# A fused transformer block on one core: the q projection of two row chunks as one Strassen pair, and a layer norm moved to ScalarE

## The chip, the cores and the metric

The kernel runs on one core of a Trainium2 chip. The metric is the device time of one execution in microseconds. Before the change it is 770.38 us, the median of 3 runs (770.19 to 770.63).

## The reference

2048 rows of 1024 numbers in bf16 go through a pre-norm block. Attention is local: each position looks at 8 positions, 2 apart, at and before itself, with 32 heads of 32. The feed-forward part is bilinear: gate times up, with no activation function between.

```python
x = A_x
h = x + _A_ref(_layernorm(x), A_wqkv, A_wo)    # x @ wqkv (1024 x 3072), attention, @ wo (1024 x 1024)
h2 = h + _B_ref(_layernorm(h), B_w_gate, B_w_up, B_w_down)   # (x @ wg) * (x @ wu), then @ wd; F = 3584
```

## The kernel before, in words

**Chunks and groups.** The rows are cut into 4 chunks of 512. `lnTs[c]` is the normalized chunk, transposed: 8 blocks (KO) of 128 channels by 512 rows. The weight wqkv comes in 6 blocks of 512 columns: blocks 0 and 1 are q, 2 and 3 k, 4 and 5 v. A *group* is `mm_group` (L429 to L432): 8 matmuls of 128x128 by 128x512 into one of the 8 PSUM banks. `qkv(c, blocks)` (L434) runs 4 groups for each block; `evac_qkv` (L342) then lets ScalarE copy the bank into a row buffer (pool `t1k`, 30 of them) and, for k and v, add the last 16 columns of the chunk before (`halo`), and SP stores it to DRAM. For q, `m` counts the 8 groups of 128 columns, and m below 8 means q.

**Attention** (`attention`, L468) is VectorE's work but for one exponential. It reads q and k back from DRAM in another order (`load_qk`, L448, issued on POOL's queue: qD, kD), later v (vD), and writes its output oD to DRAM, from where four DMAs on POOL's queue bring it back transposed as oT (L536 to L539). The chunks' attentions follow one another. `wo` of a chunk (8 groups that read oT) adds the residual row tiles `hss[c]`, and the second norm follows.

**The order of the work.** Everything is queued in the order of the program text; each engine works off its own queue in that order. TensorE's groups are written out by hand at the end of this section's listing. All else is a list of Python generators in `Background` (L37). Each `bg.step(us)`, one after each group with GROUP_US = 1.73, adds credit, up to 4; while the credit is positive, the first ready generator of the list is advanced. What it yields is charged in microseconds of VectorE's time; a pair `("later", us)` costs nothing, but puts it off. `bg.spend` charges work that is queued directly, and `bg.finish` runs a generator out. `pump`, `retire` and `state["live"]` load weight blocks in the order of `stream` into 7 buffers of pool `w`.

**The lines concerned.** Chunk 0's first block of q is done ahead of all. Then come `qkv(0, range(1, 4))`; the read of chunk 0's q and k; `qkv(1, range(4))`; v of chunk 0 and of chunk 1; `qkv(2, range(6))`; q and k of chunk 3; `wo_ln2(0)`, the output projection of chunk 0 with its second norm; v of chunk 3; and `ffn1_first`, gate and up of chunk 0, in which after 18 of 28 pairs of groups wo of chunk 1 is inserted (`wo_1`, `wo_norm`). Chunk 1's and chunk 2's first norms are `rows_gen` (statistics on VectorE, their Ln and Exp on ScalarE at L187 and L188), of which chunk 1's last two transposes are issued on ScalarE's own queue (L231). Chunk 3's first norm and chunk 1's second are `NormOnScalar` (L259): sums, squares and rows all on ScalarE. `wo_ln2` (L589) has its statistics (L183) and its normalization (L192) on VectorE.

**Strassen in the kernel.** Later stages already multiply 2x2 blocks with 7 products in place of 8 (`pair_block`, L829; the down projection from L1044 on), with f16 operands. `Scale` (L628) sums absolute weights on ScalarE and, with one matmul against ones (`total`, L642), gives each partition a power of two that keeps the f16 values in range.

Of the kernel before, what the change touches and what calls it, by code (L numbers as in the profile page):

```python
# [78 lines left out]
def kernel(  # L79
# [45 lines left out]
    bg = Background()  # L125

# [132 lines left out]
    class NormOnScalar(Norm1):  # L259
# [16 lines left out]
        def devs(self):  # L276
            nc.scalar.activation(self.nm, self.s, ACTF.Copy, scale=-1.0 / D)
            for t in range(4):
                nc.scalar.activation(self.junk[:], self.xs[t][:], ACTF.Square, bias=self.nm[:, t:t + 1],
                                     accum_out=self.ss[:, t:t + 1])  # L280
                yield "later", self.pace
            nc.scalar.activation(self.rs4[:], self.ss, ACTF.Ln, bias=eps[:], scale=1.0 / D)
# [17 lines left out]
        def rows(self):  # L300
            for t in range(4):
                self.row(t)
                self.transpose(t)
                yield "later", self.pace

# [33 lines left out]

    qkv_in = {}  # L340

    def evac_qkv(c, m, ps):  # L342
        sg = t1k.tile([128, HB + TC], BF, tag="t1k", name=f"sg{c}_{m}")
        nc.scalar.copy(sg[:, HB:HB + TC], ps[:])  # L344
# [5 lines left out]
        if m < 8:  # L350
            nc.sync.dma_start(qd[c][:, 4 * hg:4 * hg + 4, :, :].rearrange("c g d s -> (g d) c s"),
                              sg[:, HB:HB + TC].rearrange("p (c s) -> p c s", c=4))
            return
# [80 lines left out]
    def qkv(c, blocks, last=False):  # L434
        for b in blocks:
            for j in range(4):
                ps = psum.tile([128, TC], F32, tag="mm", name=f"ps{c}_{b}_{j}")
                mm_group(ps, wts["qkv", b], j, lnTs[c])
# [111 lines left out]
    class Norm2(NormOnScalar):  # L550
# [11 lines left out]
        def finish(self):  # L562
            yield from self.devs()
# [5 lines left out]
    def wo_norm(c):  # L569
# [4 lines left out]
        for t in range(4):  # L574
            for hf in range(2):
# [6 lines left out]
                if hf == 0 and t > 0:  # L582
                    n.sum(t - 1)
                bg.step(GROUP_US)
        n.sum(3)
        retire(2)
        return n

    def wo_ln2(c, at={}):  # L589
        lnT = lnTp.tile([128, KO, TC], BF, tag="lnT", name=f"lnT2_{c}")  # L590
        hs = hss[c]
        mv4, rs4 = ln_tiles(f"2_{c}")

        def norm(t):
            ln = normalize(hs[t], mv4, rs4, t)
            nc.sync.dma_start_transpose(lnT[:, :, bass.ts(t, 128)], ln[:])

        for t in range(4):
            for hf in range(2):
                ps = psum.tile([128, 512], F32, tag="mm", name=f"wo{c}_{hf}_{t}")  # L600
                for kk in range(KO):
                    nc.tensor.matmul(ps[:], lhsT=oTs[c][:, kk, t, :], rhs=wts["wo", c, hf][:, kk, :],
                                     start=(kk == 0), stop=(kk == KO - 1))
# [314 lines left out]
    def f16(ap):  # L918
        return ap.bitcast(F16)
# [434 lines left out]
```

## Time and profile before

| what | us |
| --- | --- |
| median of 3 runs | 770.38 |
| the profiled execution | 770.53 |
| its span, from the first to the last instruction | 768.7 |
| TensorE busy (3663 matmuls) | 762.8 |
| VectorE busy | 606.0 |
| ScalarE busy | 513.1 |
| GpSimd busy | 142.5 |
| matmul groups of q, k and v from 27.20 us on, without a gap | 136.41 |
| wo of chunk 0 starts | 163.61 |
| ffn1 of chunk 0 starts | 191.24 |
| wo of chunk 1 starts | 253.40 |

The span differs from the execution's time by what lies around the first and the last instruction, 1.8 us. "Idle before" and the name in brackets in a timeline say how long an engine stood still and what ended that. PE is TensorE, DVE VectorE, ACT ScalarE, POOL GpSimd, SP the engine that issues most DMAs; PEld is the load of the stationary operand, which lies beside the matmuls. A line such as L431 is the line of the kernel before.

### The profile page before, as it was taken

The numbers are of one execution on the slowest core, as the hardware profiler recorded it, in microseconds if no ns is written. First come the engines' busy times: TensorE is split into PE (matmuls) and PEld (weight loads), VectorE is DVE, ScalarE is ACT, GpSimd is POOL, SyncE is SP. The second block draws the span as 40 slices with busy tenths as digits, with TensorE's granted clock in tenths as the row PEclk, the third lists the DMA queues.
The fourth block names the chain that finished last, engine by engine and source line by source line (L and its number), as shares of the span: only waits on it lengthen the run. The fifth ranks groups of instructions, "written<-read, shape, count | busy, mean of one in ns | idle before, by whom it ended". The sixth has DMA issues, their size and how long they took to land.

```text
span 768.7 us, 10302 instructions
## 1 busy us (share of the span) xinstructions
PE 762.8 (99%) x3663; PEld 350.7 (46%) x3663; DVE 606.0 (79%) x718; ACT 513.1 (67%) x979; POOL 142.5 (19%) x152
## 2 busy tenths in 40 slices
PE   8999999999999999999999999999999999999998
PEld 5444444444444444444444444444444444444444
DVE  5639999999999999999998997975454444568863
ACT  4648966423687398778899986736777677788240
POOL 0000000200002000020000001018778677600000
PEclk9999999999999999999999999999999999999999
DMA  8999796999966699579559448674342423730001
GB/s 268 272 257 260 207 269 153 279 305 283 301 219 216 210 299 294 172 246 326 194 186 300 139 155 279 126 198 107 80 110 55 110 74 91 257 126 29 0 29 55
DMA packets 190915, 144.85 MB, mean 188 GB/s; under 512 B 81808, under 2 KB 181136, under 8 KB 188688
## 3 DMA queue, kind: packets, MB, share of 16 engines
q1 hardware_dynamic: 180416, 116.94, 54.2%
q0 software_dynamic: 3584, 22.02, 8.4%
q10 hardware_dynamic: 6864, 5.24, 2.5%
q8 instruction: 28, 0.46, 0.2%
q14 instruction: 23, 0.19, 0.1%
HBM read 110.10 MB, written 27.26 MB: 179 GB/s over the span
## 4 chain that ended last, share of the span: by engine, by line
PE 97%; DVE 2%; DMA 1%; issue 0%; ACTq 0%; DVEq 0%
PE ps L431 21%; PE dx L944 6%; PE pz L826 6%; PE pwu L431 6%; PE pu L431 6%; PE py L826 6%; PE pwg L431 6%; PE pg L431 6%; PE px L826 6%; PE wo L998 4%; PE pv L826 3%; PE ez L944 3%; PE ey L944 3%; PE ex L944 3%; PE dy L944 3%; PE wo L578 2%
## 5 line engine op out<-in xcount | busy, mean ns | idle before, releaser
L431 PE MATMUL ps<-lnT,w_qkv 128*128 128x512 bf16 x736 | 159.5, 379 | 0.0
L431 PEld LDWEIGHTS <-w_qkv 128*128 128x128 bf16 x736 | 71.9, 98 | 86.1 <-issue 0.2
L344 ACT CAST sg<-ps 128x512 bf16<-128x512 f32 x96 | 55.2, 586 | 46.9 <-PE ps L431 41.6
L477 DVE TENSOR_TENSOR prod<-qD,kD 128x4096 bf16<-128x4096 bf16 x32 | 72.2, 2284 | 12.8 <-DMA kD<-kd 12.8
L523 DVE TENSOR_TENSOR pv<-vD,at 128x4096 bf16<-128x4096 bf16 x32 | 72.4, 2285 | 0.2
L826 PEld LDWEIGHTS <-sw 128*128 128x128 f16 x448 | 43.8, 98 | 52.9 <-issue 0.2
L431 PEld LDWEIGHTS <-w_wu 128*128 128x128 bf16 x448 | 43.8, 98 | 52.9
L431 PEld LDWEIGHTS <-w_wg 128*128 128x128 bf16 x448 | 43.8, 98 | 52.9
L826 PE MATMUL px<-lnT,ws 128*128 128x512 bf16 x224 | 55.2, 379 | 0.0
L536 POOL DMA_DIRECT2D od<-oD x4 | 2.2, 544 | 275.6 <-DVE oD L534 275.6
L431 PE MATMUL pg<-lnT,w_wg 128*128 128x512 bf16 x224 | 52.9, 379 | 0.0
L431 PE MATMUL pu<-lnT,w_wu 128*128 128x512 bf16 x224 | 52.9, 379 | 0.0
L431 PE MATMUL pwu<-lnT,w_wu 128*128 128x512 bf16 x224 | 52.9, 379 | 0.0
L431 PE MATMUL pwg<-lnT,w_wg 128*128 128x512 bf16 x224 | 52.9, 379 | 0.0
L826 PEld LDWEIGHTS <-ws 128*128 128x128 f16 x336 | 32.9, 98 | 39.6
L807 POOL TENSOR_TENSOR sw<-ws 128x512 f16<-128x512 f16 x26 | 30.0, 1155 | 82.4 <-PE pv L826 49.1
L944 PEld LDWEIGHTS <-gs 128*128 128x128 f16 (+1 forms) x280 | 27.4, 98 | 33.0
L479 DVE TENSOR_TENSOR prod<-prod 128x4096 bf16<-128x4096 bf16 x16 | 36.6, 2288 | 0.4
L843 ACT COPY py<-px 128x512 f32<-128x512 f32 x28 | 16.0, 570 | 27.7 <-PE px L826 27.7
L808 POOL TENSOR_TENSOR sw<-sw,ws 128x512 f16<-128x512 f16 x26 | 30.0, 1154 | 2.0
L810 POOL TENSOR_TENSOR sw<-ws,sw 128x512 f16<-128x512 f16 x26 | 30.3, 1167 | 0.0
L809 POOL TENSOR_TENSOR sw<-ws 128x512 f16<-128x512 f16 x26 | 30.1, 1156 | 0.0
(334 smaller groups left out, 1472.9 us busy)
## 6 DMA issues: line engine op xcount, KB each, us to landing
w_wg<-in_B_w_gate_dram SPq DMA_DIRECT2D x14, 1024.0 KB, 6.9
w_wu<-in_B_w_up_dram SPq DMA_DIRECT2D x14, 1024.0 KB, 6.3
w_pair<-in_B_w_gate_dram SPq DMA_DIRECT2D x14, 512.0 KB, 4.0
w_pair<-in_B_w_up_dram SPq DMA_DIRECT2D x14, 512.0 KB, 5.3
w_wo<-in_A_wo_dram SPq DMA_DIRECT2D x6, 1024.0 KB, 7.6
w_qkv<-in_A_wqkv_dram SPq DMA_DIRECT2D x5, 1024.0 KB, 11.5
kd<-sg SPq DMA_DIRECT2D x32, 144.0 KB, 4.4
kD<-kd POOLq DMA_DIRECT2D x4, 1152.0 KB, 8.6
```

The source lines that it names most:

```text
L344: nc.scalar.copy(sg[:, HB:HB + TC], ps[:])
L431: nc.tensor.matmul(ps[:], lhsT=wt[:, ko, bass.ts(j, 128)], rhs=rhs[:, ko, :], start=(ko == 0), stop=(ko == KO - 1))
L477: nc.vector.tensor_tensor(prod[:, j], qD[:], kD[:, :, o:o + SUB], ALU.mult)
L479: nc.vector.tensor_tensor(prod[:, :, 0:16], prod[:, :, 0:16], prod[:, :, 16:32], ALU.add)
L523: nc.vector.tensor_tensor(pv[:, j], vD[:, :, o:o + SUB], at[:, w, None, :].to_broadcast((128, DH, SUB)), ALU.mult)
L807: eng.tensor_tensor(sw[:, i, 0], a21, a22, ALU.add)
L808: eng.tensor_tensor(sw[:, i, 1], sw[:, i, 0], a11, ALU.subtract)
L809: eng.tensor_tensor(sw[:, i, 2], a11, a21, ALU.subtract)
L810: eng.tensor_tensor(sw[:, i, 3], a12, sw[:, i, 1], ALU.subtract)
L826: nc.tensor.matmul(ps[:], lhsT=lhs[:, ko, :], rhs=rhs[:, ko, :], start=(fresh and ko == 0), stop=(ko == 3), skip_group_check=not fresh)
L944: nc.tensor.matmul(ps[:, bass.ds(lo, n)], lhsT=lhs[k][:, bass.ts(q, 128)], rhs=rhs[k][:, bass.ds(lo, n)], start=(fresh and k == 0), stop=( ...
L998: nc.tensor.matmul(ps[:], lhsT=oTs[c][:, kk, t, :], rhs=wts["wo", 2, hf][:, kk, :], start=(kk == 0), stop=(kk == KO - 1))
```

## The change

1. q of chunks 2 and 3 is taken out of `qkv` and computed together after wo of chunk 0 (`q_pair`, twice). The 2x2 blocks are: on the weights' side, block 0 or 1 of wqkv by the lower or upper half of the channels; on the rows' side, the half of the channels by chunk 2 or 3. For each m from 0 to 3 there are 7 products of 4 matmuls.
2. For that the q weights are converted in place to f16 with a scale (`q_abs` on ScalarE, 4 passes among the groups of chunk 0's k; `scale_q.rows`, `scale_q.total`, `q_convert`), right behind chunk 2's first norm. Their 16 block sums (`q_weight_sums`) go for m = 0 and 1 into 4 tiles of the row tiles' pool `hp`, for m = 2 and 3 into 8 row buffers of `t1k`. Chunk 1's q uses the converted weights and is scaled back in its eviction.
3. The rows' sums (`q_row_sums`) are made by VectorE during wo of chunk 0; one is written over a part of `lnTs[3]`.
4. `wo_ln2` is gone; chunk 0 uses `wo_norm(0, devs=False)`, with each row tile's sum, mean and squares on ScalarE as soon as that tile is added, and the rest in `finish(devs=False)` while the pair runs.
5. The order: chunk 1's k comes before its q; `start_attention(0)` stands ahead of the end of chunk 2's norm; loads of x of chunk 3, of weight blocks 4 and 5, and chunk 2's transposes stand behind the first block of chunk 1; chunk 3's norm is one generator (`both`). Attentions 2 and 3 are entered after the pair.

The core of the diff (`Scale` only moves up; `f16` too):

```diff
     def evac_qkv(c, m, ps):
-        nc.scalar.copy(sg[:, HB:HB + TC], ps[:])
+        if c == 1 and m < 8:
+            nc.scalar.activation(sg[:, HB:HB + TC], ps[:], ACTF.Copy, scale=scale_q.inv)
+        else:
+            nc.scalar.copy(sg[:, HB:HB + TC], ps[:])
...
+        def sum_dev(self, t):
+            col = slice(t, t + 1)
+            self.sum(t)
+            nc.scalar.activation(self.nm[:, col], self.s[:, col], ACTF.Copy, scale=-1.0 / D)
+            nc.scalar.activation(self.junk[:], self.xs[t][:], ACTF.Square, bias=self.nm[:, col],
+                                 accum_out=self.ss[:, col])
-        def finish(self):
-            yield from self.devs()
+        def finish(self, devs=True):
+            if devs:
+                yield from self.devs()
+            else:
+                yield "later", 2.0
+                self.sum_dev(3)
+                yield "later", self.pace
+                self.rstds()
+                yield "later", self.pace
             yield from self.rows()
...
-                if hf == 0 and t > 0:
+                if hf == 0 and t > 0 and devs:
                     n.sum(t - 1)
+                if hf == 1 and t > 0 and not devs:
+                    n.sum_dev(t - 1)
                 bg.step(GROUP_US)
-        n.sum(3)
+        if devs:
+            n.sum(3)
...
+    def q_abs(k):
+        if k == 0:
+            qsum["junk"] = att.tile([128, 4, 512], BF, tag="oT", name="junk_q")
+        scale_q.add(k, wts["qkv", k // 2][:, bass.ts(k % 2, 4), :], qsum["junk"][:])
+    def q_convert():
+        for r in range(2):
+            wt = wts["qkv", r]
+            nc.vector.tensor_scalar(f16(wt[:]), wt[:], scale_q.s, None, ALU.mult)
+        bg.spend(2.6)
+        bg.add(q_weight_sums(), bg.now, first=True)
...
+    def q_weight_sums():
+        for m in range(4):
+            a11, a12, a21, a22 = (q_weight(r, kh, m) for r in range(2) for kh in range(2))
...
+            nc.vector.tensor_tensor(s1, a21, a22, ALU.add)
+            nc.vector.tensor_tensor(s2, s1, a11, ALU.subtract)
+            nc.vector.tensor_tensor(s3, a11, a21, ALU.subtract)
+            nc.vector.tensor_tensor(s4, a12, s2, ALU.subtract)
+            qsum[m] = (s1, s2, s3, s4)
+            yield 1.7
+    def q_row_sums():
...
+        for k in range(4):
+            nc.vector.tensor_tensor(t1[k], b12[:, k, :], b11[:, k, :], ALU.subtract)
+            nc.vector.tensor_tensor(t2[k], b22[:, k, :], t1[k], ALU.subtract)
+            if k % 2:
+                yield 1.7
+        for k in range(4):
+            nc.vector.tensor_tensor(t4[k], b21[:, k, :], t2[k], ALU.subtract)
+        yield 1.7
+        nc.vector.tensor_tensor(t3, b22, b12, ALU.subtract)
+        yield 1.3
+    def q_product(ps, lhs, rhs, fresh):
+        for ko in range(4):
+            nc.tensor.matmul(ps[:], lhsT=lhs[:, ko, :], rhs=rhs[ko], start=(fresh and ko == 0), stop=(ko == 3),
+                             skip_group_check=not fresh)
+        bg.step(GROUP_US / 2)
...
+        for i in two:
+            xb[i] = bank("x", i)
+            q_product(xb[i], a11[i], b11, True)
+            yb[i] = bank("y", i)
+            nc.scalar.copy(yb[i][:], xb[i][:])
+        for i in two:
+            v = bank("v", i)
+            q_product(v, sw[i][0], t1, True)
+            p5[i] = room[:, m0 + i, :]
+            nc.scalar.activation(p5[i], v[:], ACTF.Copy, scale=inv)
+            q_product(yb[i], sw[i][1], t2, False)
+            zb[i] = bank("z", i)
+            nc.scalar.copy(zb[i][:], yb[i][:])
+        for i in two:
+            q_product(zb[i], sw[i][2], t3, False)
+            ub[i] = bank("u", i)
+            nc.scalar.copy(ub[i][:], zb[i][:])
+            out_vector(3, 4 + m0 + i, zb[i], p5[i])
+            q_product(xb[i], a12[i], b21, False)
+            out_scalar(2, m0 + i, xb[i])
+        for i in two:
+            q_product(ub[i], a22[i], t4, False)
+            out_scalar(2, 4 + m0 + i, ub[i])
+            q_product(yb[i], sw[i][3], b22, False)
+            out_vector(3, m0 + i, yb[i], p5[i])
...
-    qkv(0, range(1, 4))
+    qkv(0, [1])
+    qkv(0, [2], at={**to_abs(2, 0, 0), **to_abs(2, 2, 1)})
+    qkv(0, [3], at={**to_abs(3, 0, 2), **to_abs(3, 1, 3)})
     load_qk(0)
+    start_attention(0)
     bg.finish(rows2)
+    scale_q.rows()
+    qkv(1, [2], at={(2, 1): scale_q.total, (2, 2): q_convert})
+    pump(6)
+    state["live"] += 1
+    xtiles[3] = load_x(3, "x", nc.sync)
     for t in range(4):
         norm1[2].transpose(t)
-    xtiles[3] = load_x(3, "x", nc.sync)
-    pump(6)
-    state["live"] += 1
-    bg.add(norm1[3].sums(), bg.now + 18.0)
-    start_attention(0)
+    bg.add(norm1[3].both(), bg.now + 16.0, first=True)
     sums = abs_down()
-    bg.add(sums, bg.now + 25.0, first=True)
-    qkv(1, range(4))
+    bg.add(sums, bg.now + 18.0, first=True)
+    qkv(1, [3, 0, 1])
     qkv(0, range(4, 6))
     load_v(0)
-    bg.add(norm1[3].rows(), bg.now, first=True)
     qkv(1, range(4, 6))
     start_attention(1)
     pump(pair_at)
-    qkv(2, range(6))
-    start_attention(2)
+    qkv(2, range(2, 6))
     hss[0] = load_x(0, "h", nc.sync)
-    qkv(3, range(4), last=True)
+    qkv(3, range(2, 6), last=True)
     bg.finish(atts[0])
     bg.rate = 1.03
-    bg.spend(8.0)
-    nxt = wo_ln2(0)
-    qkv(3, range(4, 6), last=True)
+    bg.spend(6.0)
+    state["live"] += 1
+    rows_q = q_row_sums()
+    bg.add(rows_q, bg.now, first=True)
+    norm2 = [wo_norm(0, devs=False)]
+    bg.finish(rows_q)
+    room_q = wpool.tile([128, 4, TC], F32, tag="w", name="room_q")
+    norm2.append(norm2[0].finish(devs=False))
+    bg.add(norm2[1], bg.now, first=True)
+    for m0 in (0, 2):
+        q_pair(m0, room_q)
+    bg.finish(norm2[1])
+    retire(3)
+    lnT2_0 = norm2[0].lnT
+    start_attention(2)
     start_attention(3)
```

`out_scalar` evicts on ScalarE, `out_vector` on VectorE with p5 added, and each then stores on SP.

## The prediction, made blind

> **What bounds the kernel now.** I read the page's busy shares first, then the chain of work that ended last, then the timelines of ScalarE, POOL and VectorE around the edited stages.
>
> ```profile
> PE 762.8 (99%) x3663; PEld 350.7 (46%) x3663; DVE 606.0 (79%) x718; ACT 513.1 (67%) x979; POOL 142.5 (19%) x152
> ...
> PE 97%; DVE 2%; DMA 1%; issue 0%; ACTq 0%; DVEq 0%
> ```
>
> ```profile
> 27.20 136.41 PE ps L431 x632
> 163.61 13.81 PE wo L602 x64
> 177.42 13.81 PE ps L431 x64
> 191.24 1.73 PE pg L431 x8
> ```
>
> TensorE is the bound, and in the edited stretch it has no gap: 632 matmuls in 136.41 us are 0.2158 us each, and each stage starts when the last ends. So matmuls removed are time gained, and any wait put into TensorE's order is time lost for good. What feeds it, in the two places that the change touches:
>
> ```profile
> 29.75 2.77 ACTq L231 DMA_TRANSPOSE lnT<-ln  x2
> 32.57 0.29 ACT L187 ACTIVATE rs<-mv,eps 128x1 f32<-128x1 f32 x1 [2.70 <-issue]
> ...
> 36.99 0.29 ACT L187 ACTIVATE rs<-mv,eps 128x1 f32<-128x1 f32 x1 [0.54 <-DVE mv L184]
> ...
> 39.33 0.59 ACT L344 CAST sg<-ps 128x512 bf16<-128x512 f32 x1 [0.23 <-PE ps L431]
> ...
> 80.57 1.91 ACT L635 ACTIVATE w_ring<-w_ring 128x2048 bf16<-128x2048 bf16 x1
> ```
>
> ```profile
> 44.12 0.54 POOL L452 DMA_DIRECT2D kD<-kd  x1 [12.56 <-DMA kd<-sg]
> ...
> 136.85 0.54 POOL L536 DMA_DIRECT2D od<-oD  x1 [47.11 <-DVE oD L534]
> 141.35 3.55 POOL L539 DMA_DIRECT2D oT<-od  x4 [3.96 <-DMA od<-oD]
> ...
> 237.41 0.54 POOL L536 DMA_DIRECT2D od<-oD  x1 [63.45 <-DVE oD L534]
> 244.34 3.54 POOL L539 DMA_DIRECT2D oT<-od  x4 [6.39 <-DMA od<-oD]
> ```
>
> ```profile
> 52.34 2.29 DVE L477 TENSOR_TENSOR prod<-qD,kD 128x4096 bf16<-128x4096 bf16 x1 [12.77 <-DMA kD<-kd]
> ```
>
> ScalarE between 27 and 39 us is full: it falls behind at the two transposes and has just caught up at 39.33. Chunk 0's attention starts at 52.34, when kD lands, and kD was issued at 44.12, when the last k store of chunk 0 landed, 4.79 us after its eviction began (39.33). From there VectorE runs chunk 0's attention to 136.59 and chunk 1's to 237.37 nearly without idle time. The first quarter of oT landed at 147.9 (wo starts at 163.61) and for chunk 1 at 248.0 (wo starts at 253.40).
>
> [...] The trace agrees: the eviction at 33.00 had its matmuls done at 30.65 and stood behind the transposes. [...] The trace agrees (128x2048: 1.22 us; the scaling of 128x4096: 1.28 us), so I use its durations.
>
> **The change, part by part.** I followed the ledger of the background planner (credits, due times) through the code to see behind which matmul group each piece is queued; for before it gives the trace's order.
>
> 1. *Matmuls.* q of chunks 2 and 3 is 8 x 2 x 8 = 128 matmuls; as 4 x 7 products of 4 it is 112. f16 costs what bf16 does (0.86 us for 4 at L826). Gain 16 x 0.2158 = **-3.45 us**. The 64-column total adds up to 0.3 (512 columns: 0.32); I take 0.1. Chunk 1's q with converted weights costs nothing.
>
> 2. *The four Abs passes and the total.* Each is 128x2048 with accumulation: 1.91 us. In order on ScalarE they stand before the evictions of block 2's groups 0 and 2 and block 3's groups 0 and 1. From the trace's spacings (eviction with halo copies 0.77, Ln and Exp 0.43, transposes 2.82): 27.40 + 1.91 = 29.31; two evictions and the transpose copy to 31.34; transposes to 34.16; Ln/Exp, Abs to 36.50; eviction, Ln/Exp, eviction, Ln/Exp to 38.92; Abs to 40.83; eviction, Ln/Exp to 42.05; fourth Abs to 43.96. VectorE's two row instructions add 0.4. The total stands in TensorE's order behind chunk 1's first group, which ends at 39.29 + 1.73 = 41.02. TensorE, with all that follows it, waits from 41.0 to about 44.6: **+3.6 us** (1.9 to 4.2; the low end if the transposes were issued while evictions queued ahead of them still run; before, they began at 29.75, just after the last copy ahead of them at 29.69). [...]
>
> 3. *kD.* The last k eviction moves from 39.33 to 45.5, its store with it; with the same 4.79 and 8.2 us, kD lands at 58.5 instead of 52.34. Hidden in that wait on VectorE: the totals' small steps (0.8), 2 conversions at 1.28, 16 sums of 128x512 at 0.34: 9 us from 44.6 on, done at 54. Uncovered they would cost 9 us of attention. SP now issues w 4 and 5, x3 and chunk 2's transposes behind chunk 1's k stores, at about 51; they lie beside kD's transfer, as x3 and w did before; the slowest kD of the trace took 12.2 us instead of 8.2. The weights landed some 12.5 us after issue and are needed at 70. Chunk 3's norm, now in one piece on ScalarE, makes it some 5 us late at worst, within the banks' room.
>
> 4. *wo of chunk 0, moved 8 groups forward*: 149.8 + 3.6 = 153.4. Attention 0 ends at 58.5 + 84.25 = 142.75, oT's first quarter lands 11.4 later (136.55 to 147.95): 154.15. **+0.8 us** (0 to 5).
>
> 5. *Chunk 0's second norm on ScalarE, and the row sums.* Off VectorE go 16 half statistics, their aggregates and 4 normalizations; its stretch from 172.30 to 185.62 was 13.3 us. Now it is 8 adds at 0.61, 12 subtractions at 0.34, one at 1.15 and, in the pair, 8 outputs at 0.67: 15.5 us, plus 0.6 of waits. By the ledger 18.5 us of attention 1 precede the first add: 161.3. ScalarE then has a copy with sum 1.06, a mean 0.24 and a square 1.15 per row tile, 2.45 us: three of them run from 162.55 to 169.9, ahead of the first seed copy; the fourth (171.3 to 173.75) stands before the seed of z, Ln/Exp and biases (1.33) before the second. z can't start before 174.25 where TensorE is ready at 173.1, and its second not before 176.55 instead of 175.95: 1.15 + 0.6, and 0.1 in the second pair. **+1.8 us** (0.5 to 3). The same pattern in the later pair blocks (L826) runs at 12.09 us without a gap, but there no norm stands between the copies. The last row is transposed at about 188, behind q stores on SP that wait for VectorE's outputs; it lands 5 us later, against a start of ffn1 at 194: **+0.3** (0 to 1.5). The weight buffer kept as room delays wu 1, wg 2 and wu 2 to 195; wu 1 is needed 13.8 us later: 0. Row buffers: 8 of 30 held, 12 more for the row sums, 10 left for stores of 4 us: 0.
>
> 6. *wo of chunk 1.* VectorE's attention 1 ends at 237.37 + 6.2 (kD) + 3.2 (part 5, and one more gate product) = 246.8; oT's first quarter lands 10.7 later: 257.5. TensorE comes there at 194.3 + 62.16 = 256.5: **+1.0 us** (0 to 3). By the ledger one more piece of attention 3 (2.3 us) is left for the down projection's stage; its oT landed at 467.3, needed at 473.2: 0 (to 2). q of chunks 2 and 3 is stored by about 197, read after 201: 0.
>
> Sum: -3.45 + 0.1 + 3.6 + 0.8 + 1.8 + 0.3 + 1.0 = **+4.15 us**. The profiled execution took 770.53 (span 768.7 and 1.8 around it): 774.7; the median is 770.38, 0.15 lower: **774.5**.
>
> **The rivals.** *Faster:* the queue delay of part 2 doesn't reach the total, since the Abs passes fill waits of ScalarE (there are 2.2 us of them between 24.6 and 39.4) or run shorter. It decides from a total wait under 1.4 us with the later waits gone as well: then only 0.5 is left of the costs, 770.4 - 3.45 + 0.5 = 767.4. Against it: two of the waits are for VectorE and the passes stand behind them. *Even:* the total's wait comes as priced and hides the rest, since norm and copies are spread better than I queue them: -3.45 + 3.6 + 0.3 = 770.8. *Late kD:* it takes 12.2 us, as once in the trace; attention 0 and 1 end 4 us later, wo waits 4 more: 778.6. For it: w and x3 start beside it, at over 200 GB/s.
>
> **How the numbers follow.** Main case (772.5 to 776.5) 0.48; late kD (776.5 to 779, a little above) 0.20; even (769 to 772.5) 0.19; faster (under 768.8) 0.13. A difference under 0.2%, 1.54 us, can't be told from none here: faster 0.13, same (768.8 to 771.9) 0.16, slower 0.71. The range 768.8 to 779 leaves out the faster case and about 0.05 above.
>
> **What would show it.** Right: a TensorE gap of 3 to 4 us ahead of the total near 41; ScalarE without idle time from 27 to 46; the first attention product at 58 to 59; waits of z for ScalarE in the first pair near 175; wo of chunk 1 some 4 us later than 253.4, with oT landing last. Wrong: no gap at the total (then faster); attention's start at 52 (then part 6 costs nothing); waits in places that I put at nothing, the third attention or the weights of ffn1.

## The result and the profile after

| | us |
| --- | --- |
| median after (4 runs, 790.87 to 796.53) | 792.71 |
| median before, on the same chip | 770.43 |
| ratio after to before, 95% interval | 1.030 (1.025 to 1.034) |
| the profiled execution after, its span | 790.87, 789.1 |
| the prediction, its range | 774.5, 768.8 to 779.0 |

The change is slower, as predicted, but by 22 us where 4 were forecast. One remark on the numbers below: the profiled execution of one experiment (credit_no_abs, 783.0) is not typical of its other 13, which took 768.8 to 773.4; its trace is not used.

TensorE's timeline shows where its order stands still (start, duration, then in brackets the idle time ahead and what ended it):

```profile
39.36 1.89 PE L480 MATMUL ps<-lnT,w_qkv 128*128 128x512 bf16 x8 [0.34 <-DMA lnT<-ln]
47.45 0.23 PE L370 MATMUL l1psq<-rowbq,ones 128*128 128x64 bf16 x1 [6.20 <-DVE rowbq L365]
...
164.88 15.73 PE L644 MATMUL wo<-w_wo,oT 128*128 128x512 bf16 x63 [6.03 <-DMA oT<-od]
```

Before, the groups ran from 27.20 to 163.61 us without a gap. Now the total (L370) holds everything for 6.2 us, and wo of chunk 0 waits 6.0 us for its input. The 64 matmuls of wo also took 15.73 us, instead of 13.98 in the same view of before. The list of TensorE's waits (sum, number of times, longest) has two more:

```profile
PE qz L932 <- ACT qz L972: 1.9, 3, 1.2
PE ey L1069 <- DVE gs L1237: 1.9, 1, 1.9
```

The table of stretches explains wo's longer time. Its columns are the stretch, its length, busy time (count) of PE, PEld, DVE, ACT and POOL, then the granted clock, the DMA share and GB/s. Around the total:

```profile
44.00:46.00 2.00, 0.00 (x0) 0.00 (x0) 0.55 (x1) 1.94 (x6) 0.00 (x0) 0.89 0.26 69
46.00:48.00 2.00, 0.55 (x3) 0.28 (x4) 0.56 (x4) 1.97 (x6) 0.00 (x0) 0.50 0.02 5
...
50.00:52.00 2.00, 2.00 (x6) 0.76 (x5) 1.93 (x4) 1.01 (x4) 0.05 (x1) 0.50 0.66 148
52.00:54.00 2.00, 2.00 (x9) 0.84 (x8) 1.97 (x7) 0.46 (x2) 0.49 (x1) 0.90 0.63 111
```

During the wait the clock falls to half, and it stays there for some 5 us after the matmuls have resumed: 6 matmuls in 2 us instead of 9 or 10. The same happens at wo (0.50 from 162 to 168 us), and once more in the down projection, behind the wait of 1.9 us at 481 us:

```profile
480.00:482.00 2.00, 0.25 (x1) 0.10 (x1) 2.00 (x4) 1.94 (x5) 0.34 (x1) 1.00 0.00 0
482.00:484.00 2.00, 2.00 (x6) 0.67 (x6) 1.89 (x5) 0.70 (x2) 0.21 (x1) 0.62 0.63 262
484.00:486.00 2.00, 2.00 (x6) 0.76 (x5) 2.00 (x2) 0.00 (x0) 0.00 (x0) 0.53 0.87 332
```

Against the kernel before, stage by stage, TensorE is late by:

| term | predicted | measured |
| --- | --- | --- |
| 16 matmuls fewer | -3.45 | -3.45 |
| the total: chunk 1's second group starts at 47.68 instead of 41.03 (6.2 of it the wait, 0.2 the total itself, 0.2 a late row) | +3.7 | +6.65 |
| the clock behind that wait (wo would start at 158.84, so +9.04 in all) | none | +2.4 |
| wo of chunk 0 waits for oT | +0.8 | +6.0 |
| the clock behind that wait (15.73 against 13.81; 0.2 of it only because the first matmul now follows a wait) | none | +1.9 |
| the pair, 26.6 us for 112 matmuls (1.9 of it waits for ScalarE) | +1.8 | +2.4 |
| ffn1's start; wo of chunk 1 | +0.3; +1.0 | 0; +0.4 |
| attention 3 in the down projection (a wait of 1.9), with the clock behind it | 0 (to 2) | +4.1 |
| sum; the span's difference | +4.15 | +20.4; 20.4 |

Two chains lie behind the big terms. The first is on ScalarE, ahead of the total:

```profile
27.13 1.89 ACT L360 ACTIVATE junk_q<-w_qkv 128x2048 bf16<-128x2048 bf16 x1
...
31.07 6.07 ACTq L234 DMA_TRANSPOSE lnT<-ln  x2
37.19 0.30 ACT L190 ACTIVATE rs<-mv,eps 128x1 f32<-128x1 f32 x1 [6.01 <-issue]
...
45.02 1.89 ACT L360 ACTIVATE junk_q<-w_qkv 128x2048 bf16<-128x2048 bf16 x1
```

The first Abs pass pushed chunk 1's two transposes from 29.75 to 31.07, and there their issue took 6.07 us instead of 2.77. The second alone held ScalarE for 4.61 us, until 37.1; POOL had issued the read of qD at 30.71, and it landed 6.5 us later. The second chain is VectorE's, ahead of wo:

```profile
58.95 4.49 DVE L529 TENSOR_TENSOR prod<-qD,kD 128x4096 bf16<-128x4096 bf16 x2 [2.00 <-DMA kD<-kd]
111.31 0.69 DVE L554 TENSOR_TENSOR trs<-lg 128x512 f32<-128x512 f32 x1 [7.45 <-ACT lg L551]
```

The same wait before:

```profile
98.43 0.69 DVE L502 TENSOR_TENSOR trs<-lg 128x512 f32<-128x512 f32 x1 [1.12 <-ACT lg L499]
```

Attention 0 started when predicted (58.5), but it lasted 6.3 us longer than the 84.25 of before, because VectorE waited 7.45 us for the one exponential (before: 1.12). POOL's timeline after shows a second loss, behind attention 0:

```profile
149.73 0.54 POOL L588 DMA_DIRECT2D od<-oD  x1 [50.03 <-DVE oD L586]
158.30 3.54 POOL L591 DMA_DIRECT2D oT<-od  x4 [8.04 <-ACT sg L397]
```

oT was issued 8.6 us after od; before, 4.5 (136.85 to 141.35). The DMA view of 130 to 165 us (KB each, us to landing) shows why: the store of od took 4.2 us to land before and 8.0 after.

```profile
od<-oD POOLq DMA_DIRECT2D x1, 1024.0 KB, 4.2
od<-oD POOLq DMA_DIRECT2D x1, 1024.0 KB, 8.0
```

What made it slower was not tested; it is 8.2 us in no_abs and 6.1 in credit below.

### The profile page after: what moved, and what is told of

The parts are those of the page before. It is cut to its first block, busy times and chain, and to the rows that moved or that the text cites. A ratio compares the mean times of both kernels' runs of the same rounds, so it can differ in the third digit from the quotient of the medians.

```text
span 789.1 us, 10274 instructions
## 1 busy us (share of the span) xinstructions
PE 764.0 (97%) x3592; PEld 350.4 (44%) x3648; DVE 621.7 (79%) x748; ACT 540.3 (68%) x1017; POOL 142.4 (18%) x152
## 4 chain that ended last, share of the span: by engine, by line
PE 79%; DVE 7%; ACT 7%; DMA 3%; issue 1%; ACTq 1%; SPq 0%; POOL 0%; DVEq 0%
PE ps L480 10%; PE dx L1069 6%; PE pz L827 6%; PE py L827 6%; PE pwg L480 6%; PE pwu L480 6%; PE px L827 6%; PE pg L480 6%; PE pu L480 6%; PE wo L1123 3%; PE wo L644 3%; PE pv L827 3%; PE ez L1069 3%; PE dy L1069 3%; DMA oT<-od 2%; PE ey L1069 1%
## 5 line engine op out<-in xcount | busy, mean ns | idle before, releaser
L480 PE MATMUL ps<-lnT,w_qkv 128*128 128x512 bf16 x595 | 133.8, 384 | 1.0 <-DMA lnT<-ln 0.3
L480 PEld LDWEIGHTS <-w_qkv 128*128 128x128 bf16 (+1 forms) x608 | 59.9, 99 | 73.2 <-issue 4.0
L394 ACT CAST sg<-ps 128x512 bf16<-128x512 f32 x72 | 41.6, 585 | 25.5 <-PE ps L480 18.1
L827 PE MATMUL px<-lnT,ws 128*128 128x512 bf16 x212 | 53.1, 379 | 0.6
L808 POOL TENSOR_TENSOR sw<-ws 128x512 f16<-128x512 f16 x26 | 30.0, 1153 | 79.6 <-PE py L827 72.3
L644 PE MATMUL wo<-w_wo,oT 128*128 128x512 bf16 x126 | 29.8, 396 | 6.4 <-DMA oT<-od 6.3
```

Source lines behind the costliest of these rows:

```text
L480: nc.tensor.matmul(ps[:], lhsT=wt[:, ko, bass.ts(j, 128)], rhs=rhs[:, ko, :], start=(ko == 0), stop=(ko == KO - 1))
L808: eng.tensor_tensor(sw[:, i, 0], a21, a22, ALU.add)
L827: nc.tensor.matmul(ps[:], lhsT=lhs[:, ko, :], rhs=rhs[:, ko, :], start=(fresh and ko == 0), stop=(ko == 3), skip_group_check=not fresh)
```

## The experiments

All times are medians; ratios, with 95% intervals, are to the kernel before on the same chip. Each run has its edit, the expectation on record, and what followed.

**Where the total stands, and chunk 3's norm.** Four kernels from the changed one.

total_late: total and conversion moved behind 6 and 7 groups of chunk 1.

```diff
-    qkv(1, [2], at={(2, 1): scale_q.total, (2, 2): q_convert})
+    qkv(1, [2])
...
-    qkv(1, [3, 0, 1])
+    qkv(1, [3, 0, 1], at={(3, 2): scale_q.total, (3, 3): q_convert})
```

> The changed kernel with its total and the conversion moved six groups later (before groups 2 and 3 of the second block of chunk 1's k), so that TensorE has work until the row sums are there. Theory A (three waits that add: the total's 6.2 us and the half clock after it, some 2.5 us; attention 0 held at its exponential by chunk 3's norm; the waits of the pair and the tail): the wait at the total goes and the clock stays at 1, ScalarE's evictions and so the exponential come some 6 us earlier too, and about 6 us of the 8.7 stay gained: 784 to 787 against 791 to 796. Rival B (only attention 0's path through kD, the exponential and oT sets the end): wo of chunk 0 starts at the same 164.9 as before and the time stays at 790 to 793.

831.12 us, 1.076 (1.071 to 1.082). Both theories missed. The conversion was now queued behind attention 0's first products, which wait for kD until 58.4, so TensorE waited 13.4 us for converted weights at 67 us, and more later (12.9 us for oT). An operation that TensorE needs must not stand behind one of VectorE's that waits for a DMA.

n3_spread: chunk 3's norm queued in two steps, as before the change. n3_fill: the same, and 26 matmuls of 128x512 into a spare bank ahead of the total. n3_abs: n3_spread with the first two Abs passes two and one groups later, behind the transposes.

```diff
-    bg.add(norm1[3].both(), bg.now + 16.0, first=True)
+    bg.add(norm1[3].sums(), bg.now + 11.0, first=True)
...
+    bg.add(norm1[3].rows(), bg.now, first=True)      # behind load_v(0)
```
```diff
+        ps = psum.tile([128, TC], F32, tag="mm", name="l1psq")
+        for i in range(26):
+            nc.tensor.matmul(ps[:], lhsT=ones[:], rhs=lnTs[1][:, 0, :], start=True, stop=True)
+        scale_q.total(ps)
```
```diff
-    qkv(0, [2], at={**to_abs(2, 0, 0), **to_abs(2, 2, 1)})
+    qkv(0, [2], at={**to_abs(2, 2, 0), **to_abs(2, 3, 1)})
```

> The changed kernel with chunk 3's first norm queued as in the kernel before: its sums and squares from 7 us earlier in the planner's time, its rows after chunk 0's v. Theory A: VectorE's wait for the exponential falls from 7.4 us to 1 or 2, oT lands about 6 us earlier, and TensorE finds it there: wo of chunk 0 starts near 159 in place of 164.9, the clock stays full there, 782 to 785. Rival B says the same of this run. Rival C (the exponential is late because ScalarE is behind anyway after the Abs passes): the wait stays above 5 us and the time at 789 to 792.

> The run before this with 26 matmuls of 128x512 added ahead of the total in TensorE's order (ones by a block of chunk 1's rows, thrown away; 5.6 us of work in a wait of 6.2). It does more work and should not be slower. Theory A with the clock as a cost of its own: the granted clock stays at 1.00 from 46 to 54 us and TensorE is some 2.5 us earlier behind it, so 2 to 2.5 us faster than the run before, if oT is there by then. Rival D (the clock drop costs nothing, or comes anyway): the same time as the run before, or 0.2 more.

> The run n3_spread with the first two Abs passes moved behind the two transposes on ScalarE's queue (before groups 2 and 3 of chunk 0's first k block instead of 0 and 2). Theory A (the first pass shifts the second transpose's issue into the transfer of qD, where it takes 4.61 us instead of 1.30): the two issues take 2.8 us again, the fourth pass ends near 44 in place of 46.9, the total waits 3 to 3.6 us, and the time is 3 to 5 us below n3_spread. Rival E (the issue is slow wherever it stands): same as n3_spread within 1 us.

n3_spread: 792.14, 1.028 (1.024 to 1.032), no difference from the change. The exponential's wait fell from 7.45 to 4.20 and wo(0)'s from 6.0 to 4.2, but the end did not move; none of the three theories has both the wait and the time right. n3_fill: 788.47, 1.023 (1.020 to 1.027). The clock stayed at 1.00 and the total's wait shrank to 0.6, yet wo(0) now waited longer for oT (one wait of 7.1 us, against two of together 4.6), so in the traces most of what TensorE gained it gave back. By the medians it is 3.7 us faster than n3_spread, but the intervals overlap. n3_abs: 786.56, 1.021 (1.019 to 1.023). With the passes behind the transposes, these started at 29.73 and took 2.76 us, and the total's wait was 3.7 us: what the prediction had priced. The excess of part 2 is the stretched transpose.

**Without the Abs passes.** no_abs leaves them out; early_abs moves them, and queues chunk 3's norm in two steps as n3_spread does.

```diff
-        scale_q.add(k, wts["qkv", k // 2][:, bass.ts(k % 2, 4), :], qsum["junk"][:])
+        nc.vector.memset(scale_q.l1[:, k:k + 1], 82.0)
```
```diff
-    qkv(0, [1])
-    qkv(0, [2], at={**to_abs(2, 0, 0), **to_abs(2, 2, 1)})
-    qkv(0, [3], at={**to_abs(3, 0, 2), **to_abs(3, 1, 3)})
+    qkv(0, [1], at={**to_abs(1, 1, 0), **to_abs(1, 3, 1)})
+    qkv(0, [2, 3])
...
+    qkv(1, [2], at={**to_abs(2, 0, 2), **to_abs(2, 1, 3), (2, 2): scale_q.rows})
+    qkv(1, [3, 0, 1], at={(3, 0): scale_q.total, (3, 1): q_convert})
```

> The changed kernel without the four Abs passes on ScalarE: the partial sums are set to a constant by VectorE, so the scale no longer comes from the weights; everything else is as changed. Theory A (the passes, queued ahead of chunk 0's k evictions, are behind the total's wait, the late kD, and through kD the wait of wo(0)): TensorE's wait at the total falls from 6.2 to under 0.3 us with the granted clock at 1.00 around it; kD lands at 52 to 53 and the first attention product starts there; wo(0) waits under 1.5 us for oT; time 772 to 775. Theory B (the passes explain the total's wait only; wo(0) waits because it was moved 13.8 us forward and because od and oT now land beside v stores and weight loads): the total's wait goes too, but wo(0) waits 3 to 7 us for oT although kD is on time; time 776 to 780.

> The changed kernel with chunk 3's norm queued in two steps as before, and the Abs passes moved off the stretch from 27 to 46 us: two stand in ScalarE's order behind the first and third group of chunk 0's block 1 (17 to 25 us, where ScalarE of the kernel before has gaps of 1.4, 1.1 and 0.7 us), two behind the last k eviction of chunk 0; the total stands five groups later, the conversion six. Theory A (position in ScalarE's queue is the whole cost of the passes): no wait at the total, kD lands at 53 to 55, VectorE's conversions and weight sums end at 54 to 57 and attention 0 starts then; wo(0) waits 3 to 7 us for oT; time 776 to 782. Theory C (the passes cost ScalarE's time wherever they stand, since chunk 1's norm runs through it from 20 us on): chunk 1's normalized rows come 2 to 4 us later, TensorE waits for them or kD lands at 57 or later; time 784 to 790.

no_abs: 784.48, 1.019 (1.016 to 1.022). The total's wait went, kD was on time, and still wo(0) waited 7.0 us: VectorE waited 7.4 us for the exponential, and oT was issued 8.5 us after od. So the passes are not the cause of wo(0)'s wait, as theory A had it: the wait is there without them. Theory B named the right wait, but the time lies above its range. early_abs: 813.93, 1.052 (1.048 to 1.057). The total cost nothing (45.88 us, no wait) and conversions and sums ended at 55.3, as theory A said; but ScalarE's own load of down weights, next in its order from 103.4 on, went out only at 113.48, 10 us later (see mended below), VectorE waited 16 us for the exponential and wo(0) 12.6 for oT.

**A wait put into the kernel before.** gap6 and gap_short (a chain of 10 and of 4) make TensorE wait at 41 us and change nothing else. In short form:

```diff
+    t = att.tile([128, 2048], BF, tag="oT", name="gap_t")
+    nc.vector.memset(t[:], 1.0)
+    for i in range(10):
+        nc.vector.tensor_scalar(t[:], t[:], 1.0, None, ALU.mult)
...
+    nc.tensor.matmul(ps[:, 0:64], lhsT=ones[:], rhs=t[:, 0:64], start=True, stop=True)   # behind chunk 1's first group
```

> The kernel before, with one 64-column matmul behind chunk 1's first group that waits for a chain of 10 scalings of 128x2048 on VectorE (0.64 us each, in VectorE's idle time from 39.6 us): TensorE waits 5 to 6 us at 41 us, and nothing else is changed. Theory D (a wait of this length costs more than itself, because the granted clock falls after it): the clock is under 1.00 for 5 to 8 us behind the wait, and the end comes 2 to 3 us later than the wait explains: 777.5 to 779.5. Theory E (the low clock in the changed kernel has another reason, and a wait costs its length): clock 1.00 behind it, 775.5 to 776.6.

> As the first run with a wait put into the kernel before, but with a chain of 4 scalings (0.73 us each there) instead of 10: TensorE should wait 3.5 to 4 us at 41 us. Theory D ([...] a wait of 3.7 us is charged nearly as much clock as one of 8): the clock is under 1.00 for 3 us or more behind the wait, and TensorE's next stages come 1.5 to 3 us later than the wait explains. Theory E2 (a short wait costs its length): 0 to 0.7 us beyond the wait.

gap6: 781.28, 1.014 (1.012 to 1.015). The chain ran longer than I had reckoned:

```profile
49.25 0.23 PE L898 MATMUL gap_ps<-gap_t,ones 128*128 128x64 bf16 x1 [8.11 <-DVE gap_t L893]
...
174.78 13.98 PE L604 MATMUL wo<-w_wo,oT 128*128 128x512 bf16 x64
```

wo(0) starts 11.3 us later than before (163.45 in this view): 8.1 for the wait, 0.2 for the extra matmul and a later start, 3.0 for the clock. gap_short: 776.27, 1.007 (1.006 to 1.009); a wait of 3.8 us, wo(0) 6.9 us later, so again 3.0 for the clock in the profiled execution, and 2.0 by the medians (5.7 less 3.8). Theory D holds in both: the clock fell 3.8 us into the wait in gap6 and 2.3 us in gap_short, and was back 5.9 and 5.4 us after work had resumed. Something else shows here: in gap6 VectorE waited 11.46 us for attention 0's exponential, in gap_short 7.24, before 1.12. Nothing on VectorE or ScalarE was changed after 50 us; the exponential stands in ScalarE's order behind evictions, and these wait for TensorE. *So TensorE's lateness is passed on to attention 0.* In these two runs it cost nothing, because wo(0) came late enough.

**The second norm on ScalarE alone.** In the kernel before, `wo_ln2(0)` is replaced by the change's `wo_norm(0, devs=False)` and `finish(devs=False)`, with chunk 3's v behind it as before; norm_alone drops the `bg.spend(8.0)` ahead of it, norm_paced keeps it.

```diff
-    bg.spend(8.0)
-    nxt = wo_ln2(0)
+    nxt = wo_norm(0, devs=False)
+    fin = nxt.finish(devs=False)
+    bg.add(fin, bg.now, first=True)
     qkv(3, range(4, 6), last=True)
+    bg.finish(fin)
```

> The kernel before with one part of the change alone: chunk 0's second norm on ScalarE (sums, means and squares per row tile behind the adds, then Ln/Exp and four normalizations), with chunk 3's v groups behind it as before. Theory F (the norm on ScalarE is free or a gain where v groups and not the Strassen pair hide it): no wait ahead of ffn1 over 1 us, VectorE has 8 us less to do, time 769.5 to 771.5. Theory G (it is a cost by itself, since the last rows' sums, Ln/Exp and normalizations stand in one queue with 8 evictions): TensorE waits 1 to 4 us for the last transposed row at 191 us, time 771.5 to 775.

> The kernel before with chunk 0's second norm on ScalarE, as in the run with that norm alone, but with the planner charged 8 us ahead of wo(0) as in the kernel before, so that VectorE reaches the adds on time. Theory K (the norm's own length, from the last add to the last transposed row, is over 20 us, and the 13.8 us of v groups can't hide it where the Strassen pair's 26.6 us do): the last add ends at 181 to 182, ffn1 waits 7 to 11 us; 779 to 784 us. Theory L (the 14.6 us of the first run came from late adds): ffn1 waits under 3 us; 769 to 774.

788.03, 1.022 (1.021 to 1.024), and 787.72, 1.023 (1.021 to 1.024). ffn1 waits for the last transposed row in both; of norm_alone:

```profile
205.88 3.57 PE L434 MATMUL pg<-lnT,w_wg 128*128 128x512 bf16 x8 [14.63 <-DMA lnT<-ln]
```

In norm_paced the adds were on time (the last ended at 178.1) and the wait was 14.3 us all the same, so late adds are not the reason. From the last add to ffn1's start it is 27 us there and 21 in norm_alone (last add at 184.8): over 20, as theory K has it, with a wait longer than its 7 to 11; why the two lengths differ wasn't traced. In the change the pair's 26.6 us hide it; the v groups' 13.8 can't. Part 5's "0.3 to ffn1" was right for that reason.

**What the planner is charged.** credit: the same work, but the planner isn't charged for it.

```diff
-        bg.spend(2.6)
         bg.add(q_weight_sums(), bg.now, first=True)
...
             qsum[m] = (s1, s2, s3, s4)
-            yield 1.7
+            yield 0.1
```

> The changed kernel; the planner isn't charged for the two conversions and the weight sums (2.6 and 4 times 1.7 us before, now 0 and 4 times 0.1), which VectorE does while it waits for kD; the work itself stays. Theory P (the 9.4 us charged put attention 0's pieces, its exponential among them, behind two to four more groups in ScalarE's order, and leave pieces of attention 3 for the down projection): VectorE's wait for the exponential of attention 0 falls from 7.4 to 2 to 5 us, wo(0) waits 1 to 4 us for oT instead of 6.0, the wait of 1.9 us at 481 us goes; 784 to 789 us. Theory Q (chunk 3's norm fills ScalarE, and the place in the queue hardly matters): the exponential's wait stays over 6.5, wo(0)'s over 5, the 1.9 stays; 791 to 794.

778.24, 1.010 (1.008 to 1.011): 14.5 us less than the change, from an edit that removes no instruction. TensorE's timeline and waits:

```profile
47.51 0.24 PE L370 MATMUL l1psq<-rowbq,ones 128*128 128x64 bf16 x1 [6.12 <-DVE rowbq L365]
158.57 13.99 PE L644 MATMUL wo<-w_wo,oT 128*128 128x512 bf16 x64
```
```profile
PE qz L931 <- ACT qz L971: 0.8, 1, 0.8
```

The total's wait is unchanged. The exponential's wait is 3.59 us, od is issued at 146.18 instead of 149.73, oT 6.6 us after it instead of 8.6, and wo(0) starts with no more than 0.5 us of wait and at full clock. In the down projection nothing waits over 0.5 us: the last piece of attention 3 stands before the sums that TensorE needs, not between them. Theory P's direction holds, but its range (784 to 789) is missed, and one of its steps is smaller than it said: 47 evictions stand ahead of the exponential in ScalarE's order, 48 in the change, 47 before. The piece moved by one group of 1.73 us, not by two to four; how the rest of the 3.9 us came about was not traced.

**Putting the mends together.** mended: n3_abs with the total as in early_abs, no charge, and the down weights' sums as late as before (`bg.now + 25.0`). no_abs_mended: mended without the Abs passes, the total where the change has it. credit_abs: credit with n3_abs's passes and early_abs's total. credit_early: credit with early_abs's passes and total. credit_no_abs (and once more, credit_no_abs_again): credit without the passes. credit_abs_early_total: credit with n3_abs's passes, the total where the change has it. The edits are those above, and for mended and no_abs_mended n3_spread's and

```diff
-    bg.add(sums, bg.now + 18.0, first=True)
+    bg.add(sums, bg.now + 25.0, first=True)
```

> The changed kernel with the mends that the runs so far point to: two Abs passes behind the transposes, the total at block 3's first group and the conversion one group later, no charge for conversions and weight sums, chunk 3's norm in two steps and the down weights' sums as late as before. Theory V (VectorE's chain from kD over attention 0 to oT sets when wo(0) starts, so a wait of TensorE ahead of it that is taken away comes back there): no wait at the total, kD lands at 56, the exponential's wait is 1 to 3 us, oT's first quarter lands at 155 to 158 and wo(0) waits 5 to 8 us; 776 to 780 us. Theory W (the waits add up): wo(0) waits under 3 us, 770 to 774.

> As the mended kernel, but with the Abs passes left out (the partial sums are a constant, so the scale doesn't come from the weights) and the total and the conversion where the change has them: what the change could reach if the scale were free. Theory V: kD lands at 52 to 53, conversions and sums end at 51, attention 0 runs as in the kernel before (exponential's wait 1 to 2 us), od is issued at 137 to 138, oT's first quarter lands at 149 to 153, wo(0) waits 0 to 3 us; 769.5 to 774 us, so still no gain worth the name. Rival X (moving wo(0) 13.8 us forward costs by itself, since od lands 4 us later beside the v stores): wo(0) waits 3 to 6 us; 774 to 779.

> The run without the planner's charge, and besides the first two Abs passes behind the transposes and the total at block 3's first group with the conversion one group later (chunk 3's norm and the down weights' sums stay where the change has them). Theory V (VectorE's chain from kD over attention 0 to oT sets when wo(0) starts): no wait at the total, kD lands at 56 instead of 59, oT's first quarter lands at 155 to 156 instead of 158.5, wo(0) now waits 5 to 7 us for it; of the 9 us that the total's wait and the clock behind it cost only about 3 are gained: 775 to 777.5 us. Theory W (the waits add up): wo(0) waits under 2 us, 769 to 772.

> The run without the planner's charge, and the Abs passes as in the run with early passes (two in chunk 0's block 1, two behind the last k eviction, the total at block 3's first group). Theory V: kD lands at 52, VectorE's conversions and sums end at 55.3 and attention 0 starts there; oT's first quarter lands at 154 to 156, wo(0) waits 4 to 6 us; 774 to 777 us. Rival Y (ScalarE's load of the down weights falls into the reads of qD and kD again, as in the first run with early passes, where it was held for 10 us): the exponential waits over 10 us, 783 us or more.

> The run without the planner's charge, and the Abs passes left out (the partial sums are a constant, so the scale doesn't come from the weights): what the change is worth if the scale costs nothing. Theory V: kD lands at 52, attention 0 starts there, oT's first quarter lands at 151 to 152.5, wo(0) waits 1 to 3 us, the pair 1 us for ScalarE; 769.5 to 772 us. Rival Y (ScalarE's or SP's queue is held by the reads of qD and kD at 90 us, so that the exponential waits over 6 us): wo(0) waits over 4; 773 to 778.

> The run without the planner's charge and without the Abs passes once more, for an undisturbed trace of it: in the first one's profiled execution TensorE waited 2.9 us for a normalized row ahead of the total, which its other executions can't have done, since they were 10 us shorter. Theory V: kD lands at 52, attention 0 starts there, wo(0) waits 0.5 to 3 us for oT, no other wait of TensorE over 1 us; 769 to 771 us.

> The run without the planner's charge, with the first two Abs passes behind the transposes, but with the total where the change has it: the one combination of the mends that were tried singly which isn't measured yet. Theory V (TensorE's lateness and attention 0's chain have to match: kD lands at 56, oT's first quarter at 155 to 156, and TensorE, which waits 3.7 us at the total and loses some 2 us of clock behind it, reaches wo(0) at 155.3): wo(0) waits under 1.5 us, no wait over 1.5 us after it, 773.5 to 776 us, the best of the versions that compute their scale, and still over the kernel before. Rival Z (as in the run with a late total: ScalarE and the row buffers fall behind near 100 us, so that TensorE waits for a bank there and for oT later): 779 us or more.

| run | us | ratio (95%) | total's wait | wo(0)'s wait for oT |
| --- | --- | --- | --- | --- |
| mended | 795.64 | 1.032 (1.029 to 1.035) | 0 | 6.8 |
| no_abs_mended | 778.35 | 1.010 (1.008 to 1.012) | 0 | 3.1 |
| credit_abs | 781.59 | 1.014 (1.013 to 1.016) | 0 | 7.0 |
| credit_early | 785.91 | 1.015 (1.011 to 1.020) | 0 | 0 (4.8 for weights) |
| credit_no_abs | 770.15 | 0.999 (0.998 to 1.000) | not used | not used |
| credit_no_abs_again | 770.83 | 1.001 (0.999 to 1.002) | 0 | 0 |
| credit_abs_early_total | 775.76 | 1.009 (1.006 to 1.012) | 3.7 | under 0.5 |

mended missed both of its theories: a load of down weights came up in ScalarE's order at the wrong moment. (Whether the later sums or the norm in two steps brought it there was not run apart; mended lies 14 us above credit_abs, which has neither, and no_abs_mended 8 above credit_no_abs.) ScalarE's timeline:

```profile
100.13 0.19 ACT L360 ACTIVATION_READ_ACCUMULATOR w_ring<-w_ring 128x1 f32 x1
120.55 0.38 ACTq L672 DMA_DIRECT2D w_ring<-in_B_w_down_dram  x1
120.97 1.06 ACT L551 ACTIVATE lg<-lg 128x1024 f32<-128x1024 f32 x1 [20.64 <-DMA w_ring<-in_B_w_down_dram]
```

ScalarE stands still for 20 us before the load goes out, with the exponential behind it, and TensorE then waits 16.5 us for ScalarE. All that while POOL's reads of chunk 1's q and k are under way, issued at 91.7 and 92.2. Of the DMA view, from 88 to 122 us (KB each, us to landing):

```profile
kD<-kd POOLq DMA_DIRECT2D x1, 1152.0 KB, 27.8
qD<-qd POOLq DMA_DIRECT2D x1, 1024.0 KB, 24.9
```

Before, the two landed after 12.2 and 9.4 us. no_abs_mended has the same in small (3.4 us), and lies above theory V's range, in the one of rival X (wait 3.1, time 778.35; its runs go from 774.5 to 794.9). But credit_no_abs has wo(0) at the same place in the order and takes 770.15 us, so the place alone doesn't cost that much. In credit_abs the total is free, and wo(0) waits 7.0 us: the wait comes back there, as V said, with 2.5 more for a bank at 102 us that V hadn't (its time is above V's range, in none of W's). credit_early scatters from 776.4 to 787.7, and V's time was wrong too. In its trace the exponential waits only 2.2 us, but the hold that rival Y feared is there. It came one step later, behind the exponential:

```profile
105.51 0.19 ACT L360 ACTIVATION_READ_ACCUMULATOR w_ring<-w_ring 128x1 f32 x1
117.33 0.37 ACTq L672 DMA_DIRECT2D w_ring<-in_B_w_down_dram  x1
```

So the evictions stood still for 12 us and TensorE waited 8.9 us for one of them at 119 us. Why some executions are 10 us shorter stays open. credit_no_abs came out in V's range: with the scale for nothing and nothing charged, the change is worth nothing that can be measured. credit_no_abs_again has its median in V's range, but its profiled execution (774.5) waited 3.0 us for a row at 39 us, which V excluded and which I had taken for a peculiarity of the first one; attention 0 started at 54.87, not 52. credit_abs_early_total came out as V said:

```profile
44.76 0.20 PE L370 MATMUL l1psq<-rowbq,ones 128*128 128x64 bf16 x1 [3.74 <-DVE rowbq L365]
155.26 13.98 PE L644 MATMUL wo<-w_wo,oT 128*128 128x512 bf16 x64
```

TensorE reaches wo(0) at 155.26, where oT is there, and wo runs at full clock. It is the best version that computes its scale, and still slower than the kernel before. No run beats the kernel before.

Four of the kernels differ in two things alone, the passes and the charge (medians, us):

| | with the passes | without |
| --- | --- | --- |
| charged | 792.71 (the change) | 784.48 (no_abs) |
| not charged | 778.24 (credit) | 770.15, 770.83 (credit_no_abs, again) |

The charge costs 14.5 us with the passes and 14 without; the passes cost 8.2 us with the charge and 7.4 to 8.1 without. Within the runs' scatter (some 6 us among the executions of the change and of no_abs) the two add, and together they are the whole loss.

## Why the prediction was wrong, step by step

- **Part 1** (-3.45 for 16 matmuls) held, as far as the sum of the stages shows it: with this term the stages add up to the span's difference.
- **Part 2** (+3.6): the mechanism was right, the size not. The step that failed was taking 2.82 us for the two transposes "from the trace's spacings". Moved 1.3 us later they took 6.07 us. Where the passes stand behind them (n3_abs, credit_abs_early_total) the wait is 3.7. With nothing charged, that brings wo(0) from 158.57 to 155.26 us, and the median from 778.24 to 775.76, though the intervals overlap.
- **No term for the clock.** Every wait was priced at its length. The two gap runs put 2 to 3 us on top of one, at 3.8 us as at 8.1. In these traces the clock falls to half at a wait (0.50): it fell 2.3 us (gap_short), 3.8 us (gap6) and 4.3 us (the change) into the wait at 41 us, worked out from the means of the stretches. The wait of 1.9 us at 481 us was followed by half clock too, from 482.5 on, and so were five of the six like it in other runs. In n3_abs, a wait of 3.7 us at 41 us had the clock at 0.50 while one of 3.9 us at wo(0) left it at 1.00; what decides between the two was not shown.
- **Part 3**, "Hidden in that wait on VectorE ... 9 us", is where the prediction failed most. The work was hidden, as said (attention 0 started at 58.95, predicted 58.5). The step that failed is that the prediction put all else about this work at nothing, its charge too: the planner counts 2.6 + 4 x 1.7 = 9.4 us for it and queues other pieces later. The exponential (by one group) and the pieces of attention 3 in the tail came late by it. credit shows what it cost: 14.5 of the 22 us. That edit alone brings wo(0)'s wait to 0.5 us at the most, the pair's waits from 1.9 to 0.8 (and 0.3 elsewhere in it), and the tail's 4.1 us to nothing. The prediction speaks of "the ledger", and follows it to find where pieces are queued in the change; it never asks what the ledger holds back.
- **Part 4** (+0.8, "0 to 5") took attention 0's 84.25 us over unchanged. It lasted 90.5 us. How far the exponential's wait comes from TensorE's lateness (gap runs), from the charge (credit: -3.9) and from chunk 3's norm in one piece (n3_spread: -3.25) isn't a sum: the three queue each other. Beyond the wait's 6.3 us, oT was issued 8.6 us after od, not 4.5, since od took 8.0 us to land: the 11.4 us from attention 0's end to oT's first quarter, taken over from before, became 15.4.
- **Part 5**: the pair's waits of 1.21, 0.52 and 0.22 us for ScalarE answer to 1.15, 0.6 and 0.1. Right, and the norm's hiding behind the pair too.
- **Part 6**: wo of chunk 1 waited 0.4 (predicted 1.0). For the tail "0 (to 2)" was wrong by 4.1: pieces of attention 3 stood between the down projection's sums on VectorE. It was listed as a place to look at, with too low a price.
- **The rivals.** "Late kD" named the largest loss, 778.6, still 14 us short, and not the reason: kD landed 6.9 us after its issue, sooner than the 8.2 of part 3. The time of "even" is what is left when the passes are free and nothing is charged, but not for its reason, a total's wait that hides the others. All cases took one wait at a time; none had waits that make the next one longer.

The theory that stands: the change saves 3.45 us and spends them on waits that it makes itself. Of the 22 us over the kernel before, 14.5 are the charge in the planner and some 8 the Abs passes: some 2.5 of these the stretched transpose, some 5 what they cost even in the better place (775.76 against 770.15 and 770.83). Without both, the saving is used up by the pair's 1.2 us and small waits; no run takes this rest apart. What a pair ahead of wo(0) would do wasn't tried: the second norm would then stand uncovered.

## What to carry to other kernels

Work that is hidden in a wait can still cost, through whatever counts it: look at what a scheduler charges for it, and at who is queued later for that. Price a wait of TensorE of some 2 us or more at its length and some 2 to 3 us for the clock (2.0 to 3.0 in the gap runs, 2.4 and 1.9 in the change; behind three of the 38 such waits here the clock stayed full, and behind none of 1.5 us or less did it fall), and follow its lateness through the evictions into the other engines' order. Before moving an operation on an engine that also issues DMAs, look at what is in flight where it lands (moved 1.3 us later, two transposes took 6.07 us to issue instead of 2.77).

## What the runs showed of the hardware

- A DMA's issue can hold the engine that issues it for far longer than usual, and where that was looked at (before, the change, early_abs, credit_early and mended) a large read of POOL's was in flight meanwhile: a transpose on ScalarE's queue 4.61 us instead of 1.3; one on SP's 8 to 12 us in every version but mended (before too: 11.09 at 91.21), and 20.47 there. Ahead of a plain load on its queue ScalarE stood still for 10 us (early_abs), 12 (credit_early) and 20 (mended). That the reads are the cause isn't shown, and why some issues are held and their neighbours (1.26 us) aren't stays open.
- The clock fell 2.2 to 5.1 us after a wait of TensorE had begun, in some runs only when work had resumed, and was back 2.7 to 5.9 us after that. A wait of 8.1 us cost hardly more of it than one of 3.8. In the traces used, from 24 us on, it fell behind 6 of 7 waits of 1.9 us and behind all but two of the 31 longer ones (2.5 us in credit_abs, 3.9 in n3_abs).
